# The last 96 rows of w_down move from ACT's queue at the start to Sync's queue behind load 17, in three loads on 16, 5 and 3 DMA engines

## The chip, the cores and the metric

The kernel runs on one core of a Trainium2 chip. The core has five engines with an instruction stream each: PE (matmuls; its weight loads are shown as PEld), DVE (vector work), ACT (scalar functions), POOL, and SP, here called Sync, which only issues transfers. Sixteen DMA engines move the data between memory (HBM) and the core's on-chip memory (SBUF). To keep the two kinds apart, the sixteen are always called DMA engines.

The metric is the device time of one execution in microseconds (us), the median over several runs.

## The reference

One decoding step for two rows of x (B = 2, D = 512). The rows are normalised (layernorm without weights), and three things are added: x itself, an attention over the last 2048 cached positions of 32 heads, and a gated linear block.

```python
x = A_x
xn = _layernorm(x, axis=-1)
# attention: q = xn @ wq per head; k, v = the last W = 2048 rows of the caches
scores = jnp.einsum("bhqd,bhkd->bhqk", q, k) * (Dh ** -0.5)
p = _softmax(scores, axis=-1)
o = jnp.einsum("bhqk,bhkd->bhqd", p, v)          # then @ wo
# linear block, F = 1376
h = (xn @ w_gate) * (xn @ w_up)
y = h @ w_down
return x + attention + y
```

All is float32. The caches alone are 2 x 32 x 2048 x 128 x 4 bytes for k and as much for v, 134 MB; with the weights the kernel reads 159 MB, and each byte is used once.

w_down has 1376 rows of 512 numbers (2 KB each). They are used in ten blocks of 128 rows and a rest of 96 rows. The change is about this rest, 196 608 bytes.

## The kernel before

**The stream.** The host lays caches and weights out as one long array, in the order in which the kernel wants them. The function `loads()` lists what is in each load: load 0 (constants and the first part of wq), load 1 (k of heads 0 to 2 and wq), load 2 (w_gate and w_up), loads 3 to 22 (three tiles of k or v each, 16 KB per partition, and up to three pieces of wq, wo or w_down), load 23 (v of head 30) and load 24 in five parts (v of head 31, pieces of wo, and w_down's blocks 1 to 9). A full load is 128 partitions of 13 824 numbers, 6912 KB. They go into three buffers `step0` to `step2` in turn; loads 0 and 23 go into `extra`.

**What sets the order.** A small recorder (`Program`) notes every operation with what it writes and reads; `emit` then writes each engine's instructions in the order in which the code named them, and adds the semaphore waits. There is no scheduler. Every operation is therefore recorded at one line, L198 of the profile (L197 for separate waits), and tiles, not lines, tell the operations apart.

All loads are issued on Sync, in the order of `queue`. `issue(n)` issues everything in the queue up to load n; a load waits on Sync until its buffer's last readers are done. Each DMA engine works off its own shares of the queued loads in order. Each load has a semaphore of its own.

**The steps.** For each head k is multiplied by q on DVE (`step<-step,q`, 4.4 us) and summed on DVE (`s<-step`, 4.4 us); for each group of four heads `weights` forms the softmax's weights (`mt`, `both`, `tr`, `nm`, `p`), and PE multiplies v with them (`o_ps<-step,p`). When a group is done, ACT copies its sums (`o_sb`), PE gathers them (`gu<-cst,o_sb`), DVE scales them (`oT`), and PE multiplies them with wo into `acc`. The loop `for n in range(3, 21)` does this load by load. `turn` (in step 3) puts the linear block's h into `hT`, 128 values to a column; PE multiplies its columns with the blocks of w_down, some in the loop and most at the very end, while load 24's parts land.

**The rest of w_down.** It has a buffer of its own, `wr`, 96 partitions of 512 numbers. It is loaded from a separate array, `wd_rest`, by ACT, right after Sync's first four loads have been recorded; behind it ACT issues the load of `xr`, the two rows of x as they are (2 partitions of 512). The product of `wr` with the last 96 values of h (`acc<-wr,hT`) is in `turn`.

Of the kernel before, what the change touches and what calls it, by code (L numbers as in the profile page):

```python
# [10 lines left out]
P = 128  # L11
B, D, H, DH, SK, F = 2, 512, 32, 128, 8192, 1376
# [7 lines left out]
NFC = F // P  # L20
FR = F - NFC * P
# [9 lines left out]
BUFS = 3  # L31
WIDTH = 13824
WIDTH_X = 4096


def loads():
# [199 lines left out]
def build(nc, stream, x_nat, wd_rest, out):  # L236
    pr = Program(nc)
    pe, dve, act, pool = pr.pe, pr.dve, pr.act, pr.pool

    buf = [pr.sb(f"step{i}", [P, WIDTH]) for i in range(BUFS)]  # L240
    buf_x = pr.sb("extra", [P, WIDTH_X])
    xr = pr.sb("xr", [P, D])
    wr = pr.sb("wr", [FR, D])
# [20 lines left out]
    hT = pr.sb("hT", [P, 4, NFB, B])  # L264
# [10 lines left out]
    got, used, queue, pos = {}, {}, [], 0  # L275
    for n, t, fields in loads():
        tile = buf_x if t == "x" else buf[t]
        c0 = used.get(n, 0)
        for kind, i, w in fields:
            c = used.get(n, 0)  # L280
            got[kind, i] = tile[:, c : c + w]
            used[n] = c + w
        c1 = used[n]
        assert c1 <= tile.shape[1], (n, c1)
        src = stream[pos : pos + P * (c1 - c0)].rearrange("(p i) -> p i", p=P)
        pos += P * (c1 - c0)
        queue.append((n, tile[:, c0:c1], src))

    def issue(upto):
        while queue and queue[0][0] <= upto:  # L290
            _, dst, src = queue.pop(0)
            pr.load("SP", dst, src)

    issue(3)
    pr.load("ACT", wr, wd_rest)
    dve.memset(mean_w, 1.0 / D)
    dve.memset(eps_t, EPS)
    dve.memset(ones, 1.0)
# [55 lines left out]
    def products(h):  # L354
        g, hh = divmod(h, HG)
        kt, qb = keys(h), q_ps[g % 2][:, hh * DH : (hh + 1) * DH]
        dve.tensor_tensor(kt, kt, qb.unsqueeze(1).to_broadcast([P, J, DH]), op=ALU.mult)

    def sums(h):
        g, hh = divmod(h, HG)  # L360
        dve.tensor_reduce(s_t[g % 2][:, hh, :], keys(h), axis=AX.X, op=ALU.add)
# [29 lines left out]
    def denominators(g):  # L391
        dve.tensor_reduce(
            rs, own(p_all[:, g % 2, 0, 0, 0:4], (HG, B, JG, 4)), axis=AX.XY, op=ALU.add
        )

    def reciprocals(g):
        dve.reciprocal(rec[g % 2], tot)

    def weigh(h, bank=None, first=None, last=None):
        g, hh = divmod(h, HG)  # L400
        bank = g % 2 if bank is None else bank
        first = hh == 0 if first is None else first
        last = hh == HG - 1 if last is None else last
        v = got["v", h]
        for i in range(JG):
            j = 32 * (i % 4)
            pe.matmul(
                o_ps[bank][j : j + M, :], p_all[:, g % 2, hh, i, :],
                v[:, i * FB : (i + 1) * FB],
                start=(first and i < 4), stop=(last and i >= JG - 4),  # L410
            )

    def fold(g):
        act.copy(o_sb[g % 2], o_ps[g % 2])

    def gather(g, lo=0, hi=N):
        for r in range(4):
            pe.matmul(
                pk_ps[:, lo:hi], o_sb[g % 2][:, r * DH : (r + 1) * DH], pick[:, r, lo:hi],
                start=(r == 0), stop=(r == 3),  # L420
            )

    def scaled(g, lo=0, hi=N):
        dve.tensor_tensor(
            oT[g % 2][:, lo:hi], pk_ps[:, lo:hi], rec[g % 2][:, lo:hi], op=ALU.mult
        )
# [5 lines left out]
    def add_rows(lhsT, rhs, j, last=False):  # L432
        pe.matmul(
            acc[32 * j : 32 * j + B, :], lhsT, rhs, start=(n_acc[j] == 0), stop=last
        )
        n_acc[j] += 1
# [33 lines left out]
    def turn():  # L470
        dve.tensor_copy(
            hT.rearrange("p i n b -> p (i n b)"), hT_ps[:, 0 : 4 * B * NFB]
        )
        add_rows(hT[:FR, NFC % 4, NFC // 4, :], wr, 0)

    def down(c, add, *args, **kw):
        add(hT[:, c % 4, c // 4, :], got["wd", c], *args, **kw)

    def wo(h, add, *args, **kw):
        g, hh = divmod(h, HG)  # L480
        add(oT[g % 2][:, B * hh : B * hh + B], got["wo", h], *args, **kw)
# [16 lines left out]
    def has(n, kind):  # L498
        return [i for k, i, _ in plan.get(n, []) if k == kind]
# [19 lines left out]
    def projections(done):  # L519
        while open_q and (open_q[0][1][0] - 2) * HG + HG - 1 <= done:  # L520
            project(*open_q.pop(0)[1])

    for n in range(3, 21):
        ks, vs = has(n, "k"), has(n, "v")
        for h in late_wo:
            wo(h, add_rows, h % HG)
        late_wo = []
        full = None
        for h in vs:
            if n > 3:  # L530
                weigh(h)
            if h % HG == HG - 1:
                full = h // HG
                fold(full)
        open_q += [(n, i) for i in has(n, "wq")]
        projections(ks[0] - 1)
        for c in has(n, "wd"):
            down(c, add_rows, 1)
        if full is not None:
            gather(full)  # L540
        for x, h in enumerate(ks):
            products(h)
            if open_g is not None:
                denominators(open_g)
                open_g = None
            if n == 3 and x == 0:
                turn()
            projections(h)
            sums(h)
            if n == 20 and x == 1:  # L550
                weigh(25)
                weigh(26)
            if h % HG == HG - 1:
                weights(h // HG)
                open_g = h // HG
                if open_g:
                    reciprocals(open_g - 1)
            if x == 0 and full is not None:
                scaled(full)
                for i in range(full * HG, full * HG + HG):  # L560
                    if i in has(n, "wo") or i in has(n - 1, "wo"):
                        wo(i, add_rows, i % HG)
                    else:
                        late_wo.append(i)
        if n == 3:
            weigh(vs[0])
        if n < 20:
            issue(min([n] + [m - 1 for m, _ in open_q]) + 3 + (n == 19))

    g = NG - 1  # L570
    a, b, c, d = GROUPS[g]
# [31 lines left out]
def laid_out(x):  # L603

    import numpy as np

    a = x["A_x"].reshape(B, D)
    xs = np.zeros((P, CX), a.dtype)
    xs[:, : B * NC] = a.reshape(B, P, NC).transpose(1, 0, 2).reshape(P, B * NC)
    o = B * NC  # L610
    for r in range(4):
        for n in range(N):
            xs[4 * n + r :: 32, o + r * N + n] = 1.0
    o += 4 * N
    for n in range(HG):
        for q in range(4):
            xs[32 * q + n, o + 4 * n + q] = 1.0
    o += 4 * HG
    for n in range(NFB):
        for b in range(B):  # L620
            xs[32 * n + b, o + n * B + b] = 1.0
    o += 2 * NFB
    for j in range(4):
        for b in range(B):
            xs[32 * j + b, o + b] = 1.0
    xs[:, o + 2 :] = a[:, 0]
    cache = {
        kind: x[name][:, :, SK - W :, :].reshape(B, H, HB, J * DH).transpose(1, 0, 2, 3)
        for kind, name in (("k", "A_k_cache"), ("v", "A_v_cache"))
    }  # L630
    wq = x["A_wq"].reshape(P, NC, H * DH)
    wo = x["A_wo"].reshape(H, P, D)
    gu = {
        kind: x[name].reshape(P, NC * F)
        for kind, name in (("wg", "B_w_gate"), ("wu", "B_w_up"))
    }
    wd = x["B_w_down"]

    def field(kind, i):
        if kind == "c":  # L640
            return xs
        if kind in ("k", "v"):
            return cache[kind][i].reshape(P, CK)
        if kind == "wq":
            g, c = i
            return wq[:, c, g * HG * DH : (g + 1) * HG * DH]
        if kind == "wo":
            return wo[i]
        if kind == "wd":
            return wd[i * P : (i + 1) * P]  # L650
        return gu[kind]

    parts = [
        np.concatenate([field(kind, i) for kind, i, _ in fields], axis=1).ravel()
        for _, _, fields in loads()
    ]
    return {"stream": np.concatenate(parts), "x": a, "wd_rest": wd[NFC * P :]}


_INS = ["A_x", "A_k_cache", "A_v_cache", "A_wq", "A_wo", "B_w_gate", "B_w_up", "B_w_down"]  # L660
# [24 lines left out]
```

## Time and profile before

| | |
|---|---|
| median of 3 runs | 377.47 us (377.38 to 377.53) |
| the profiled execution | 377.64 us |
| its span, first to last instruction | 376.3 us |
| moved by DMA in the span | 159.66 MB, mean 424 GB/s |
| busy: PE, DVE, ACT, POOL | 189.3, 302.8, 14.5, 2.6 us |
| load of `wr`: size, issue to landing | 192 KB, 5.5 us |
| a full load: issue to landing (median of 17) | 31.2 us |

The profile is that of one execution. Its 0 is the first instruction's start. In the timeline a row has start, duration, engine, line, operation, written tile, read tiles, shape, count, and in brackets the engine's idle time ahead of it with what ended it; `SPq` and `ACTq` are the queues' issuing instructions. In the chain of waits a row has start, duration and what the end of the kernel was waiting for in that time. The DMA view of a window counts the packets that start in it, by size and by queue; a queue's row has packets, MB and the time that its packets took as a share of 16 DMA engines over the window. A DMA engine that has finished its share of a load writes 4 bytes, and these count as packets too.

### The profile page before, as it was taken

What the parts mean: (1) busy time and instruction counts of PE and PEld (TensorE: products, weight loads), DVE (VectorE), ACT (ScalarE), POOL (GpSimd) and SP (SyncE); (2) the same over time, 40 slices, a digit from 0 to 9 for tenths busy, and PEclk for the clock granted to TensorE, in tenths of its full rate; (3) what the DMA queues carried; (4) which work ended last, traced back from release to release, by engine and by line L of the source; (5) the groups of instructions that cost most, each with busy time, mean ns of one, the idle gap of its engine ahead of it and who ended that gap; (6) DMA issues with size and microseconds to landing.
All of it is one profiled execution on the core that took longest, in us unless ns stands there. A gap on an engine that the chain in (4) does not pass through costs nothing.

```text
span 376.3 us, 1954 instructions
## 1 busy us (share of the span) xinstructions
PE 189.3 (50%) x844; PEld 56.8 (15%) x844; DVE 302.8 (80%) x165; ACT 14.5 (4%) x28; POOL 2.6 (1%) x9
## 2 busy tenths in 40 slices
PE   0651747703762355617446383462657335243976
PEld 0210122100220011102121020110111012000312
DVE  3059979999999988899599499969969997999401
ACT  1000100000000000000000000000000001000100
POOL 2000000000000000000000000000000000000000
PEclk9956966876665658768555856858566685565999
DMA  8999899998999989999999999999999999999995
GB/s 324 470 394 488 376 470 411 431 470 377 464 435 417 464 382 460 453 400 464 394 448 453 406 458 400 447 454 406 453 420 419 445 447 434 441 402 411 432 416 235
DMA packets 4443, 159.66 MB, mean 424 GB/s; under 512 B 498, under 2 KB 626, under 8 KB 980
## 3 DMA queue, kind: packets, MB, share of 16 engines
q1 hardware_dynamic: 4320, 159.35, 98.5%
q10 hardware_dynamic: 116, 0.20, 0.1%
q8 instruction: 6, 0.10, 0.1%
q14 instruction: 1, 0.01, 0.0%
HBM read 159.49 MB, written 0.07 MB: 424 GB/s over the span
## 4 chain that ended last, share of the span: by engine, by line
DMA 49%; DVE 42%; PE 6%; issue 2%; another core or an unknown queue 1%; SPq 0%; DVEq 0%
DMA step<-in_stream_dram 49%; DVE step L198 22%; DVE s L198 19%; PE q L198 3%; PE o_ps L198 2%; PE acc L198 2%; PE tr L198 0%; DVE both L198 0%; DVE nm L198 0%; DVE h_sb L198 0%; DVE rec L198 0%; SPq L198 0%; DVE mt L198 0%; DVE o_out L198 0%
## 5 line engine op out<-in xcount | busy, mean ns | idle before, releaser
L198 DVE TENSOR_TENSOR step<-step,q 128x4096 f32<-128x4096 f32 x32 | 141.1, 4408 | 37.3 <-DMA step<-in_stream_dram 37.3
L198 DVE TENSOR_REDUCE s<-step 128x32 f32<-128x4096 f32 x32 | 141.4, 4418 | 0.8
L198 PE MATMUL o_ps<-step,p 128*32 128x512 f32 x496 | 94.8, 869 | 69.8 <-DMA step<-in_stream_dram 68.2
L198 PE MATMUL q<-step,xnb 128*128 128x512 f32 x56 | 41.4, 877 | 26.9 <-DVE step L198 19.7
L198 PE MATMUL acc<-step,oT 128*2 128x512 f32 x64 | 23.6, 926 | 42.2 <-DVE oT L198 28.5
L198 PEld LDWEIGHTS o_ps<-step,p 128*32 128x32 f32 x496 | 20.4, 147 | 126.8 <-DMA step<-in_stream_dram 74.9
L198 PEld LDWEIGHTS q<-step,xnb 128*128 128x128 f32 x56 | 13.4, 267 | 54.5 <-DVE step L198 24.9
L198 ACT ACTIVATE p<-s,zero 64x128 f32<-64x128 f32 x16 | 6.4, 399 | 268.1 <-DVE s L198 268.0
L198 DVE TENSOR_TENSOR oT<-gu,rec 128x8 f32<-128x8 f32 x8 | 1.3, 158 | 14.8 <-PE gu L198 14.8
L198 PE MATMUL tr<-both,ones 128*128 128x24 f32 (+1 forms) x18 | 4.8, 348 | 15.7 <-DVE both L198 15.7
L198 PE MATMUL gu<-step,xn 128*2 128x512 f32 (+1 forms) x48 | 8.5, 647 | 7.5 <-DMA step<-in_stream_dram 7.5
L198 PE MATMUL gu<-cst,o_sb 128*128 128x8 f32 x64 | 10.1, 285 | 3.1 <-ACT o_sb L198 3.1
L198 PEld LDWEIGHTS gu<-cst,o_sb 128*128 128x128 f32 x64 | 9.4, 225 | 10.6 <-ACT o_sb L198 8.9
L198 PEld LDWEIGHTS acc<-step,oT 128*2 128x2 f32 x64 | 1.5, 82 | 53.0 <-DVE oT L198 29.1
L198 PEld LDWEIGHTS tr<-both,ones 128*128 128x128 f32 x18 | 3.8, 262 | 26.6 <-DVE both L198 26.6
L198 PE MATMUL q<-extra,xnb 128*128 128x512 f32 x8 | 6.2, 947 | 1.9 <-DVE xnb L198 1.9
L198 DVE TENSOR_REDUCE nm<-tr 64x4 f32<-64x8 f32 x16 | 2.6, 163 | 5.4 <-PE tr L198 5.3
L198 ACT COPY o_sb<-o_ps 128x512 f32<-128x512 f32 x8 | 4.7, 585 | 46.0 <-PE o_ps L198 46.0
L198 PE MATMUL gu<-cst,h_sb 128*128 128x6 f32 x8 | 1.9, 362 | 5.6 <-DVE h_sb L198 5.6
L198 PE MATMUL tr<-st,mean_w 128*128 128x4 f32 x2 | 0.6, 365 | 7.5 <-DVE st L198 7.5
L198 PEld LDWEIGHTS gu<-step,xn 128*2 128x2 f32 x48 | 2.0, 93 | 14.7 <-DMA step<-in_stream_dram 9.1
L198 DVE TENSOR_REDUCE both<-p 128x8 f32<-128x256 f32 x8 | 3.3, 413 | 0.6 <-ACT p L198 0.6
(52 smaller groups left out, 39.8 us busy)
## 6 DMA issues: line engine op xcount, KB each, us to landing
step<-in_stream_dram SPq DMA_DIRECT2D x17, 6912.0 KB, 31.2
step<-in_stream_dram SPq DMA_DIRECT2D x2, 6400.0 KB, 29.5
step<-in_stream_dram SPq DMA_DIRECT2D x1, 6656.0 KB, 35.9
step<-in_stream_dram SPq DMA_DIRECT2D x1, 5504.0 KB, 34.4
step<-in_stream_dram SPq DMA_DIRECT2D x1, 4608.0 KB, 23.8
extra<-in_stream_dram SPq DMA_DIRECT2D x1, 2048.0 KB, 28.3
step<-in_stream_dram SPq DMA_DIRECT2D x1, 2048.0 KB, 24.8
step<-in_stream_dram SPq DMA_DIRECT2D x2, 1024.0 KB, 19.6
```

Of the source, the lines that this page charges most:

```text
L198: ins = getattr(e, method)(*args, **kw)
```

## The change

The load of `wr` is taken from ACT. Behind load 17 three loads are put into Sync's queue instead: rows 0 to 31, viewed in memory as 16 times 2 rows, rows 32 to 56 as 5 times 5, and rows 57 to 95 as 3 times 13. The first dimension sets over how many DMA engines a load is spread. The host lays the rows out so that each lands in its old place. The product with `wr` is taken from `turn` and comes at step 19 of the loop, behind the products with v and ahead of the gather.

```diff
+REST_AT = 17
+REST = ((16, 32), (5, 25), (3, 39))
...
         queue.append((n, tile[:, c0:c1], src))
+        if n == REST_AT:
+            lo = 0
+            for k, m in REST:
+                src = wd_rest[lo : lo + m, :].rearrange("(j i) d -> i j d", i=k)
+                queue.append((n, wr[lo : lo + m, :], src))
+                lo += m
...
     issue(3)
-    pr.load("ACT", wr, wd_rest)
     dve.memset(mean_w, 1.0 / D)
...
         dve.tensor_copy(
             hT.rearrange("p i n b -> p (i n b)"), hT_ps[:, 0 : 4 * B * NFB]
         )
-        add_rows(hT[:FR, NFC % 4, NFC // 4, :], wr, 0)
...
         for c in has(n, "wd"):
             down(c, add_rows, 1)
+        if n == REST_AT + 2:
+            add_rows(hT[:FR, NFC % 4, NFC // 4, :], wr, 0)
         if full is not None:
             gather(full)
...
-    return {"stream": np.concatenate(parts), "x": a, "wd_rest": wd[NFC * P :]}
+    rest, lo = [], NFC * P
+    for k, m in REST:
+        rest.append(wd[lo : lo + m].reshape(k, m // k, D).transpose(1, 0, 2).reshape(m, D))
+        lo += m
+    return {"stream": np.concatenate(parts), "x": a, "wd_rest": np.concatenate(rest)}
```

Sync's transfers around load 17, before. The row with x15 ends with load 17; the rows under it are loads 18 to 21.

```order
L198 DMA step<-in_stream_dram 128x13824 x15
L198 DMA step<-in_stream_dram 128x12800
L198 DMA step<-in_stream_dram 128x13824
L198 DMA step<-in_stream_dram 128x12800
L198 DMA step<-in_stream_dram 128x13312
```

The same place after the change.

```order
L200 DMA step<-in_stream_dram 128x13824 x15
L200 DMA wr<-in_wd_rest_dram 32x1x512
L200 DMA wr<-in_wd_rest_dram 25x1x512
L200 DMA wr<-in_wd_rest_dram 39x1x512
L200 DMA step<-in_stream_dram 128x12800
```

Three loads of `wr` stand between loads 17 and 18, and none on ACT.

PE at step 19, before: the softmax's sums of step 18 (`tr`), step 19's products with v (`o_ps`), the gather (`gu<-cst,o_sb`), the products with wo (`acc<-step,oT`), and step 20's first products.

```order
L198 MATMUL tr<-both,ones 128x24
L198 MATMUL o_ps<-step,p 32x512 x8
L198 MATMUL gu<-cst,o_sb 128x8 x4
L198 MATMUL acc<-step,oT 2x512 x4
L198 MATMUL o_ps<-step,p 32x512 x24
```

The same place after the change.

```order
L200 MATMUL tr<-both,ones 128x24
L200 MATMUL o_ps<-step,p 32x512 x8
L200 MATMUL acc<-wr,hT 2x512
L200 MATMUL gu<-cst,o_sb 128x8 x4
L200 MATMUL acc<-step,oT 2x512 x4
```

The product with `wr`, one matmul of the program that the profile shows as two, stands between the products with v and the gather; in step 3 it is gone.

## The prediction

> **What bounds the kernel now.** I read the DMA queues first, then the chain of waits from its end backwards, then the DMA in small windows.
>
> ```profile
> q1 hardware_dynamic: 4320, 159.35, 98.5%
> q10 hardware_dynamic: 116, 0.20, 0.1%
> q8 instruction: 6, 0.10, 0.1%
> q14 instruction: 1, 0.01, 0.0%
> ```
>
> q1 is Sync's queue (packets, MB, share of the time of 16 DMA engines in the span): the stream fills 98.5%. q10 is ACT's: the 96 rows that are moved and the two rows of x. q8 and q14 fetch instructions: seven packets.
>
> The chain of waits, its later part (start, duration, who):
>
> ```profile
> 248.34 34.23 DMA step<-in_stream_dram
> ...
> 309.05 35.85 DMA step<-in_stream_dram
> ...
> 350.90 22.78 DMA step<-in_stream_dram
> 373.68 0.04 issue
> 373.72 0.66 PE q L198 x16
> 374.38 0.02 issue
> 374.41 0.29 DVE o_out L198
> ```
>
> The last load (512 KB) is issued at 350.90 and lands at 373.68: it stood 20 us in the queue. What follows is 16 matmuls, a copy and the store. So the end is set by the bytes queued on the DMA engines, provided the queue is never empty. The closest it comes to that is load 4, from the timeline:
>
> ```profile
> 44.56 5.29 SPq L198 DMA_DIRECT2D step<-in_stream_dram  x2
> 52.34 4.42 DVE L198 TENSOR_TENSOR step<-step,q 128x4096 f32<-128x4096 f32 x1 [2.25 <-DMA step<-in_stream_dram]
> ```
>
> Load 4 is issued at 44.56, and load 3 ahead of it lands only at 52.3 (DVE's wait ends there): 7.8 us of cover, the smallest of all loads. Nothing that the compute engines do within a microsecond moves the end.
>
> But "the queue" is sixteen. A load is cut into sixteen equal shares, and each DMA engine works off its own shares in order. Each reports a share with a 4-byte write, which the DMA view counts under "under 512 B". Four windows: around load 4's landing (67.70 to 68.25), two around that of load 24's first part (363.20 to 363.75, 364.60 to 365.20), and the last reports of all (372.60 to 373.30; the wait for them ends 0.4 us later, at 373.68):
>
> ```profile
> DMA packets 32, 0.88 MB, mean 1609 GB/s; under 512 B 16, under 2 KB 16, under 8 KB 16
> DMA packets 29, 0.22 MB, mean 402 GB/s; under 512 B 9, under 2 KB 9, under 8 KB 9
> DMA packets 34, 0.22 MB, mean 369 GB/s; under 512 B 7, under 2 KB 7, under 8 KB 7
> DMA packets 21, 0.06 MB, mean 82 GB/s; under 512 B 7, under 2 KB 7, under 8 KB 21
> ```
>
> At load 4 all sixteen report within half a microsecond. Late in the run nine report, and seven more come over a microsecond later. Seven is also the number of instruction packets above. The DMA view from 68 to 72 us shows one of these:
>
> ```profile
> q8 instruction: 1, 0.02, 1.7%
> ```
>
> 1.7% of 16 engines in 4 us is 1.09 us of one engine. Such a fetch pushes back one DMA engine's share for good, and since no packet of the stream ever waits for work, it never catches up. At the end the others idle (stretch, its length, then each engine's busy time; the last two numbers are the DMA share and GB/s):
>
> ```profile
> 361.00:362.00 1.00, 1.00 (x12) 0.26 (x8) 0.00 (x0) 0.00 (x0) 0.00 (x0) 1.00 0.96 410
> 371.25:371.50 0.25, 0.25 (x4) 0.00 (x0) 0.00 (x0) 0.00 (x0) 0.00 (x0) 1.00 1.05 426
> 371.50:372.00 0.50, 0.16 (x4) 0.00 (x0) 0.27 (x1) 0.00 (x0) 0.00 (x0) 1.00 0.50 197
> 372.00:372.50 0.50, 0.02 (x4) 0.03 (x8) 0.42 (x1) 0.00 (x0) 0.00 (x0) 1.00 0.42 172
> 372.50:373.00 0.50, 0.50 (x20) 0.48 (x24) 0.00 (x0) 0.00 (x0) 0.00 (x0) 1.00 0.34 139
> ```
>
> From 371.5 on the share is 0.50, 0.42, 0.34: seven engines of sixteen (0.44) carry the last 1.5 us. The time of the kernel is that of the latest DMA engine, not of the mean.
>
> **The change part by part.** Before, the 96 rows of 2 KB go out from ACT at the start, six to each DMA engine, between the packets of load 0. The timeline's row, and the queues from 2 to 7 us:
>
> ```profile
> 0.73 0.41 ACTq L198 DMA_DIRECT2D wr<-in_wd_rest_dram  x1
> DMA packets 263, 2.06 MB, mean 412 GB/s; under 512 B 34, under 2 KB 34, under 8 KB 132
> q10 hardware_dynamic: 116, 0.20, 11.3%
> ```
>
> q10's 116 packets are 96 + 2 rows and 16 + 2 reports, so x's load of two rows ran on two DMA engines. *Price of a row:* 11.3% of 16 engines in 5 us is 9.04 us, over 98 rows 0.092 us, with the reports and a small overlap in it: the upper bound. The lower is the bytes alone: 410 to 426 GB/s over 16 engines, quoted above, is 26 GB/s each, 0.077 us for 2 KB. I take 0.080, near the lower end, since single packet records put the next packet that long after a row's start.
>
> *New shares.* 32 rows on 16 engines are 2 each; 25 on 5 are 5; 39 on 3 are 13. If the small loads use the same end of the row of engines (an assumption; the only load on few engines before is x's), three engines get 2 + 5 + 13 = 20 rows, two get 7, eleven get 2. Against 6 each: +14 rows (+1.12 us), +1 row (+0.08 us), -4 rows (-0.32 us). [...]
>
> *Who is late.* Followed from packet to packet (on one engine the next begins 3 or 4 ns before the one ahead ends), the records of the two engines that carry x's rows show no instruction fetch. They are among the nine: they make their last report at about 371.66 and 371.80, the latest engine at 373.24. With +1.12 the later of them ends at 372.92. The latest engine, if it is not favoured, ends at 373.24 - 0.32 = 372.92. Both put the end 0.32 earlier. With 0.092 a row the favoured engine ends at 373.09 and the gain is 0.15; with 0.077 it is 0.31. I take 0.31.
>
> *The start.* All engines begin the stream without six rows between load 0's packets: loads 0 to 17 land 0.48 us earlier, which pays nothing by itself, since the rows come back behind load 17. Sync's issues (shortest, median, longest, ns):
>
> ```profile
> L198 SPq DMA_DIRECT2D step<-in_stream_dram x27: 327/328/679, 1.2 to 350.9; - x27
> ```
>
> Three more of these are 1.0 to 2.0 us of Sync, right behind load 17's issue, without a wait and with the queue covered by at least 7.8 us: free, and without that cover 2 us late. ACT issues one less.
>
> *The product moves* from the turn of h in step 3 to step 19. There it must wait for all three loads, and the gather stands behind it on PE. Timeline, step 3 (three rows) and step 19 (four rows):
>
> ```profile
> 56.91 1.86 PE L198 MATMUL acc<-wr,hT 96*2 96x512 f32 x2 [2.47 <-DVE hT L198]
> 62.04 0.23 DVE L198 TENSOR_SCALAR both<-cst,mc 128x16 f32<-128x16 f32 x1
> 62.33 0.62 PE L198 MATMUL tr<-both,ones 128*128 128x24 f32 x2
> ...
> 314.08 3.64 PE L198 MATMUL o_ps<-step,p 128*32 128x512 f32 x16 [3.32 <-DMA step<-in_stream_dram]
> 317.79 0.58 ACT L198 COPY o_sb<-o_ps 128x512 f32<-128x512 f32 x1 [5.48 <-PE o_ps L198]
> 318.43 1.88 PE L198 MATMUL gu<-cst,o_sb 128*128 128x8 f32 x8 [0.70 <-ACT o_sb L198]
> 323.05 0.15 DVE L198 TENSOR_TENSOR oT<-gu,rec 128x8 f32<-128x8 f32 x1
> ```
>
> In step 3 PE is rid of 1.86 us ahead of a product that waits for DVE until 62.27 anyway: at most 0.1 us of DVE's time, and none at the end. In step 19 the rows have landed for some 30 us (load 17, ahead of them, lands at 282.6 by the chain). The product takes up to 1.86 us from 317.8; 0.70 of it is PE's idle time, so the gather ends 1.2 us later, near 321.5; DVE, busy until 323.05, is what the next step waits for. Free, with 1.5 us of cover; without it 1.2 us late on DVE, which has 7.8 us to the DMA.
>
> *Sum.* -0.31 for the shares, 0 for the start, the issues and the product. The profiled execution took 377.64 (span 376.3), 0.17 above the median; the same difference on the median of 377.47 gives 377.16, on the profiled execution 377.33.
>
> **A rule against the change.** The last parts of load 24 land back to back in PE's waits, and the store shows a lone small transfer:
>
> ```profile
> 360.76 1.92 PE L198 MATMUL o_ps<-extra,p 128*32 128x512 f32 x16 [1.27 <-DMA extra<-in_stream_dram]
> 365.65 1.93 PE L198 MATMUL o_ps<-step,p 128*32 128x512 f32 x16 [1.26 <-DMA step<-in_stream_dram]
> out_dram<-o_out SPq DMA_DIRECT2D x1, 64.0 KB, 1.6
> ```
>
> 2048 KB in 365.65 - 360.76 = 4.89 us is 429 GB/s: a load behind another pays no fixed time. If each small load did block its engines for the store's 1.6 us, the three engines that serve all three loads would end 4.8 - 0.48 = 4.3 us later and the kernel, less their 1.44 us of room, some 2.9 us: 380.4. [...] The row of 429 GB/s speaks against it for queued loads.
>
> **The rivals.**
> *The third favoured engine is a late one (slower).* x shows two of the three engines. The third is one of the other fourteen, seven of which are late. By their last reports (372.74 to 373.24) plus 1.12 the end would be 373.86 to 374.36: 0.62 to 1.12 later, 378.1 to 378.6, over the bound of change from about +0.75. It decides as soon as that engine has had a fetch. For it: by count alone 7 in 14. Against it: the seven fetches hit seven different engines, which chance would do in one of five cases, so they go round in an order; q8's six on neighbours that spare the first two engines have nine places to begin, one of which includes the third, and q14's one falls on it once in fourteen. I give it 0.15.
> *Little or nothing is gained.* One of the two engines with 7 rows is a late one: it ends at 372.82 to 373.32, and the kernel at 377.16 to 377.55. 0.08.
> *Each small load has a fixed price*, 380.4: 0.03.
> *More is gained.* The stream's opening (2.06 MB in 5 us) is held up by ACT's rows for more than their bytes, up to another half microsecond: 376.6. Against it: 412 GB/s there is what the stream does later. 0.05.
>
> **How the numbers follow.** Forecast 377.16 with 0.69; its own range, by the price of a row and the spread of the times shown (377.38 to 377.53), is 377.0 to 377.4. The range for 8 in 10 reaches to the lower part of the first rival: 376.9 to 378.1. A measurement of this kernel can tell about 0.2% (0.75 us) from no change, so the forecast counts as no change. Faster: the last rival, and a little more for its mechanism beside the forecast's, 0.07. Slower: three quarters of the first rival (five of the seven late engines are late enough) and the fixed price, 0.15. Within: 0.78.
>
> **What would show it.** After the change, load 0's wait on DVE ends about 0.4 us earlier; q10 has 4 packets instead of 116; behind load 17 Sync issues three loads of wr; from 371.5 on the DMA share stays near 1 for longer and falls within some 0.2 us, with the last report near 372.9. If the third engine is late, one engine alone reports a microsecond behind the others and the share ends in a tail of 0.06. If the rows cost more, three engines are last. The forecast is wrong if an instruction fetch lands on a favoured engine, or if a load on three engines does not use x's two.

## The result: 0.56 us slower, small but clear of the noise, and the profile after

| | before | after |
|---|---|---|
| median of 21 runs | 377.47 us (377.32 to 377.72) | 378.03 us (377.74 to 378.32) |
| the profiled execution | 377.64 us | 377.83 us |

The ratio is 1.0014, with a 95% interval from 1.0008 to 1.0020. The interval lies above 1, so the kernel is slower, by about 0.15%. The profiled execution of after is one of its shorter ones, 0.20 below its median, and that of before 0.17 above its own, so the two traces differ by 0.19 us where the medians differ by 0.56. What is read below are parts of the traces that differ by a microsecond.

The queues of the changed kernel (packets, MB, share):

```profile
q1 hardware_dynamic: 4440, 159.55, 98.7%
q8 instruction: 6, 0.10, 0.1%
q14 instruction: 1, 0.01, 0.0%
q10 hardware_dynamic: 4, 0.00, 0.0%
```

The rows have left ACT's queue, which has x's four packets. Sync's has 120 more, 96 rows and 24 reports, and 24 is 16 + 5 + 3: the loads ran on as many DMA engines as their first dimensions have. The fetches are still seven. The end of the chain of waits, after:

```profile
351.04 22.81 DMA step<-in_stream_dram
373.85 0.04 issue
373.89 0.66 PE q L200 x16
374.55 0.02 issue
374.58 0.29 DVE o_out L200
```

The end has the same form as before and the last load lands at 373.85 instead of 373.68. The timeline's waits for loads 0, 15, 17 and 18, before:

```profile
6.64 0.20 DVE L198 COPY cst<-extra 128x66 f32<-128x66 f32 x1 [3.83 <-DMA extra<-in_stream_dram]
...
249.90 4.42 DVE L198 TENSOR_TENSOR step<-step,q 128x4096 f32<-128x4096 f32 x1 [3.55 <-DMA step<-in_stream_dram]
...
282.59 4.42 DVE L198 TENSOR_TENSOR step<-step,q 128x4096 f32<-128x4096 f32 x1 [3.34 <-DMA step<-in_stream_dram]
...
297.73 1.94 PE L198 MATMUL o_ps<-step,p 128*32 128x512 f32 x8 [7.79 <-DMA step<-in_stream_dram]
```

And the same four, after:

```profile
5.75 0.20 DVE L200 COPY cst<-extra 128x66 f32<-128x66 f32 x1 [2.94 <-DMA extra<-in_stream_dram]
...
248.91 4.42 DVE L200 TENSOR_TENSOR step<-step,q 128x4096 f32<-128x4096 f32 x1 [3.55 <-DMA step<-in_stream_dram]
...
282.55 4.42 DVE L200 TENSOR_TENSOR step<-step,q 128x4096 f32<-128x4096 f32 x1 [4.29 <-DMA step<-in_stream_dram]
...
297.87 1.94 PE L200 MATMUL o_ps<-step,p 128*32 128x512 f32 x8 [9.07 <-DMA step<-in_stream_dram]
```

A row's start is the landing of the load it waited for. Without the rows the start is 0.89 us earlier (6.64 to 5.75), and load 15 still 0.99 us. At load 17 the lead has shrunk to 0.04, and at load 18 after is 0.14 behind. So all that the start gave, and a little more, is lost around the rows' new place. The 8 us around it, before and then after (length, busy time of PE, PEld, DVE, ACT, POOL, then PE's clock, DMA share, GB/s):

```profile
276.00:284.00 8.00, 4.33 (x22) 1.51 (x26) 4.66 (x3) 0.11 (x1) 0.00 (x0) 0.62 1.00 432
```

```profile
276.00:284.00 8.00, 2.74 (x14) 0.54 (x18) 3.71 (x3) 0.00 (x0) 0.00 (x0) 0.68 0.93 343
```

The DMA engines are busy in both (1.00 and 0.93), but they move 343 GB/s instead of 432. A packet counts with all its bytes where it starts, so such a window is rough: begun a microsecond later it gives 392 against 420. The landings above say more exactly what is lost. The DMA engines have work nearly throughout (1.03 from 277 to 287 us); their packets take longer.

The tail of after, and the last reports of all (the DMA view from 373.05 to 373.50):

```profile
371.50:372.00 0.50, 0.32 (x4) 0.00 (x0) 0.12 (x1) 0.00 (x0) 0.00 (x0) 1.00 0.83 336
372.00:372.50 0.50, 0.00 (x0) 0.00 (x0) 0.50 (x1) 0.00 (x0) 0.00 (x0) 1.00 0.69 279
372.50:373.00 0.50, 0.37 (x16) 0.36 (x20) 0.08 (x1) 0.00 (x0) 0.00 (x0) 1.00 0.64 262
373.00:373.50 0.50, 0.50 (x28) 0.38 (x16) 0.00 (x0) 0.00 (x0) 0.00 (x0) 1.00 0.27 107
```

```profile
DMA packets 21, 0.05 MB, mean 100 GB/s; under 512 B 10, under 2 KB 10, under 8 KB 21
```

The share stays high for longer than the 0.50, 0.42, 0.34 of before, and ten DMA engines report last, within 0.45 us: the seven that had a fetch, and three with 20 rows each (from the packet records, followed one after another on each DMA engine). The balance is the computed one; it is reached later.

Single packet records show what slowed. Each group is of one size, so that a longer time is not more bytes (ns; from the records, which the views sum up):

```
                                   before       after         without rows anywhere (first experiment)
load 0's packets, 8456 B, median      370         320         320
a row's packet, 2048 B, median         84         127         -
load 18's first packet on each of
the 16 DMA engines, 51 200 B    1891-1898   2042-2885   1891-1898
```

Before, the rows begin at 2.7 us. Beyond each DMA engine's first packet, load 0's packets still take 320 ns for the first microsecond beside the rows, and some 320 to 400 ns from 3.75 us on. Without rows they stay at 320. After, every one of the sixteen DMA engines has a slow packet behind load 17, also the eleven that carry only two rows.

### The profile page after: what moved, and what is told of

Read it like the earlier page. It is cut to its first block, busy times and chain, and to the rows that moved or that the text cites. A ratio compares the mean times of both kernels' runs of the same rounds, so it can differ in the third digit from the quotient of the medians.

```text
span 376.5 us, 1956 instructions
## 1 busy us (share of the span) xinstructions
PE 187.2 (50%) x844; PEld 55.5 (15%) x844; DVE 302.8 (80%) x165; ACT 14.5 (4%) x28; POOL 2.6 (1%) x9
## 4 chain that ended last, share of the span: by engine, by line
DVE 49%; DMA 48%; PE 2%; SPq 1%; issue 0%
DMA step<-in_stream_dram 48%; DVE s L200 24%; DVE step L200 23%; PE acc L200 1%; DVE both L200 1%; PE tr L200 1%; SPq L200 1%; DVE mt L200 0%; DVE nm L200 0%; DVE mtt L200 0%; DVE mc L200 0%; PE q L200 0%; DVE rec L200 0%; DVE oT L200 0%; DVE o_out L200 0%
## 5 line engine op out<-in xcount | busy, mean ns | idle before, releaser
L200 PE MATMUL o_ps<-step,p 128*32 128x512 f32 x496 | 96.9, 888 | 70.2 <-DMA step<-in_stream_dram 68.6
L200 PE MATMUL q<-step,xnb 128*128 128x512 f32 x56 | 38.6, 823 | 31.5 <-DVE step L200 23.6
L200 PE MATMUL gu<-step,xn 128*2 128x512 f32 (+1 forms) x48 | 9.4, 712 | 8.1 <-DMA step<-in_stream_dram 8.1
L200 PE MATMUL gu<-cst,o_sb 128*128 128x8 f32 x64 | 9.3, 271 | 2.4 <-ACT o_sb L200 2.4
L200 PEld LDWEIGHTS gu<-cst,o_sb 128*128 128x128 f32 x64 | 8.6, 208 | 9.8 <-ACT o_sb L200 8.0
```

The lines of the kernel that those rows point to most:

```text
L200: ins = getattr(e, method)(*args, **kw)
```

## The experiments

Each run is set against the kernel before on the same chip, whose median was 377.50, 377.52 and 377.51 in the three groups. Two readings serve: the median, and, for rows that come behind load 17, the time from load 15's landing to load 18's, from waits like those above (before, with no rows there, 297.73 - 249.90 = 47.83; after 297.87 - 248.91 = 48.96). The table at the end of this section has both.

### What the rows cost at all

Without the three loads and the product.

```diff
-        if n == REST_AT:
+        if False:
...
-        if n == REST_AT + 2:
-            add_rows(hT[:FR, NFC % 4, NFC // 4, :], wr, 0)
```

> The changed kernel without the three loads of wr and without their product (the last 96 values of h are left out of the result). It gives the floor: what the 96 rows cost in either place. If rows cost only their own 0.08 us each (the prediction's price, 6 to a DMA engine), the time is 0.48 under the kernel before: 377.0. If they also hold up the stream beside them by what load 0 showed (its reports came 0.75 to 0.83 us earlier without them), it is 376.65 to 376.7.

Measured: 376.72 (376.66 to 377.00), ratio 0.9978 [0.9969, 0.9987].

```profile
5.74 0.20 DVE L200 COPY cst<-extra 128x66 f32<-128x66 f32 x1 [2.92 <-DMA extra<-in_stream_dram]
...
248.98 4.42 DVE L200 TENSOR_TENSOR step<-step,q 128x4096 f32<-128x4096 f32 x1 [3.33 <-DMA step<-in_stream_dram]
...
281.65 4.42 DVE L200 TENSOR_TENSOR step<-step,q 128x4096 f32<-128x4096 f32 x1 [3.33 <-DMA step<-in_stream_dram]
...
296.80 2.79 PE L200 MATMUL o_ps<-step,p 128*32 128x512 f32 x12 [7.58 <-DMA step<-in_stream_dram]
```

This is the floor. Up to load 15 it goes like after; load 17 lands 0.90 and load 18 1.07 us earlier. The rows' own bytes, 196 608 at the stream's 424 GB/s, are 0.46 us if all engines share them. They cost 377.50 - 376.72 = 0.78 at the start and 378.03 - 376.72 = 1.31 behind load 17. In both places they cost more than their bytes, and the records above show packets beside them that are slowed.

### Where the source lies in memory

The first idea for it: 96 neighbouring rows of 2 KB are one small region of memory, on which all engines read at once. Here the rows lie 55 296 B apart, in after and in before.

```diff
-                src = wd_rest[lo : lo + m, :].rearrange("(j i) d -> i j d", i=k)
+                src = wd_rest[lo : lo + m, 0:D].rearrange("(j i) d -> i j d", i=k)
...
+    rows = np.concatenate(rest)
+    apart = np.zeros((FR, WIDTH), rows.dtype)
+    apart[:, :D] = rows
```

> As the changed kernel, but in memory each row of wd_rest stands 55 296 bytes from the next instead of 2048. Theory A (rows close together in memory: DMA engines that read them at once are held up at one place, and the stream's reads with them): the rows go back to 84 ns each, the stream's packets beside them to 1.9 to 2.05 us, and the time falls by about 0.9 to 377.1. Theory B (the rows' destination: partitions that other DMA engines write) and theory C (any run of 2 KB packets slows the DMA engines): nothing changes, 378.0.

Measured: 378.04 (377.87 to 378.14), ratio 1.0013 [1.0004, 1.0021]; the rows' packets still take up to 167 ns.

```diff
-    pr.load("ACT", wr, wd_rest)
+    pr.load("ACT", wr, wd_rest[:, 0:D])
...
+    apart = np.zeros((FR, WIDTH), wd.dtype)
+    apart[:, :D] = wd[NFC * P :]
```

> The kernel before, but in memory each row of wd_rest stands 55 296 bytes from the next. Theory A: load 0's packets beside the rows stay at 320 ns instead of 380, load 0 lands 0.3 us earlier, and the time is 377.1 to 377.2. Theories B and C: 377.47.

Measured: 377.53 (377.42 to 378.13), ratio 1.0003 [0.9994, 1.0012]. Both stay where they were: how close the rows lie in memory is not it.

### One load on sixteen engines

Perhaps the loads on few DMA engines did it. The same 96 rows, behind load 17, as one load of six rows to each engine:

```diff
-REST = ((16, 32), (5, 25), (3, 39))
+REST = ((16, 96),)
```

> As the changed kernel, but the 96 rows behind load 17 are one load on 16 DMA engines, six rows each. Theory A: the rows are still close together, but three DMA engines no longer read neighbouring rows in step: it is held up as at the start of the kernel before, 377.4 to 377.6. Theory C: 96 small packets as before, 377.5. If it is the few DMA engines with many rows each that do the harm: only 6 x 0.08 = 0.48 over the floor, 377.1 to 377.2.

Measured: 378.22 (377.89 to 378.47), ratio 1.0018 [1.0009, 1.0027]. None of the expectations was near it. It is no better than the three loads, so spreading over few engines is not what costs. One transfer is not cheaper than three, as a fixed price for each load would make it; that it is 0.19 dearer is not clear of the noise, since the two intervals overlap.

### Who writes which partitions

Left were the destination and small packets as such. A load of the stream always has 128 partitions; this one has 96. With 128 rows, 32 of them zero, the load has the stream's 128 partitions. That each DMA engine then writes the partitions that it writes in the stream is the author's assumption, and no trace shows it.

```diff
-    wr = pr.sb("wr", [FR, D])
+    wr = pr.sb("wr", [P, D])
...
-            lo = 0
-            for k, m in REST:
-                src = wd_rest[lo : lo + m, :].rearrange("(j i) d -> i j d", i=k)
-                queue.append((n, wr[lo : lo + m, :], src))
-                lo += m
+            queue.append((n, wr, wd_rest))
```

> The rest of w_down behind load 17 as one load of 128 rows of 2 KB (the 96, and 32 rows of zeros, 64 KB more) to all 128 partitions, in the natural order, so that it has the stream's own shape. Theory A is out, since rows apart in memory cost as much. Theory B (rows that a DMA engine writes to other partitions than those it writes in the stream hold up all): each DMA engine now writes the partitions that it writes in the stream, so nothing is held up; 8 rows of 0.08 us over the floor of 376.72 is 377.36. Theory C (2 KB packets as such slow the DMA engines): 128 of them do at least what 96 did, 378.0 to 378.4.

Measured: 377.39 (377.14 to 377.45), ratio 0.9996 [0.9987, 1.0005].

```profile
248.79 4.42 DVE L200 TENSOR_TENSOR step<-step,q 128x4096 f32<-128x4096 f32 x1 [3.56 <-DMA step<-in_stream_dram]
...
281.48 4.42 DVE L200 TENSOR_TENSOR step<-step,q 128x4096 f32<-128x4096 f32 x1 [3.34 <-DMA step<-in_stream_dram]
...
297.31 1.93 PE L200 MATMUL o_ps<-step,p 128*32 128x512 f32 x8 [9.05 <-DMA step<-in_stream_dram]
```

```profile
276.00:284.00 8.00, 3.68 (x18) 0.79 (x22) 4.66 (x3) 0.00 (x0) 0.00 (x0) 0.68 1.02 434
```

A third more rows, and 0.64 us less than after. Load 17 isn't held up (281.48 - 248.79 = 32.69, as in before, against 33.64 in after), the 8 us keep 434 GB/s, and all 128 row packets take 84 to 88 ns. So packets of 2 KB as such are not slow. The cost, 377.39 - 376.72 = 0.67, is about what 262 144 B take at 424 GB/s, 0.62.

The same 128 rows as 512 more columns of load 18, so that there is no extra load:

```diff
-        18: wq(7, 3),
+        18: wq(7, 3) + units("wd", 10),
```

> The same 128 rows (32 of zeros), but as 512 more columns of load 18, so that they are part of its packets of 51 200 bytes, which become 53 248: no packet of 2 KB and no load of its own. Theories B and C alike: 8 x 2 KB at the stream's rate, 0.60 to 0.64 over the floor, 377.3 to 377.4. If more, it is neither the rows' destination nor their size but the bytes at this place.

Measured: 377.32 (377.22 to 377.39), ratio 0.9995 [0.9986, 1.0003], a cost of 0.60: the extra load itself costs next to nothing.

And the 128 rows in the kernel before, at the start on ACT:

```diff
-    wr = pr.sb("wr", [FR, D])
+    wr = pr.sb("wr", [P, D])
...
+    rest = np.zeros((P, D), wd.dtype)
+    rest[:FR] = wd[NFC * P :]
```

> The kernel before, with the load of wr on ACT at the start as 128 rows (32 of zeros) to 128 partitions. Theory B: no packet of load 0 is held up (320 ns all through), 8 x 0.08 over the floor: 377.36, under the kernel before although it moves 64 KB more. Theory C: 0.78 x 128 / 96 = 1.04 over the floor, 377.76.

Measured: 377.31 (377.16 to 377.65), ratio 0.9996 [0.9987, 1.0005], a cost of 0.59 where the 96 rows cost 0.78. The interval holds 1, so the times alone don't tell the two apart; the trace does.

```profile
6.34 0.20 DVE L198 COPY cst<-extra 128x66 f32<-128x66 f32 x1 [3.53 <-DMA extra<-in_stream_dram]
```

With a third more bytes the first wait ends 0.30 us earlier than before's 6.64, and nearly all of load 0's packets stay at 320 ns.

128 rows differ from 96 in the number of rows too. This run keeps the 128 rows, their packets and their place behind load 17, and changes the view by which they are dealt out: 16 times 8, by which each DMA engine should be given eight neighbouring partitions. The host stores the rows in another order to match, so that each lands in its old place.

```diff
-            queue.append((n, wr, wd_rest))
+            src = wd_rest.rearrange("(j i) d -> i j d", i=16)
+            queue.append((n, wr, src))
```

> As the kernel with one load of 128 rows behind load 17 (377.39), with one difference: its source is viewed as 16 times 8 rows, as the change views its first load, so that each DMA engine should take 8 partitions in a row instead of those that it writes in the stream. Same bytes, same packets, same partitions in all. Theory B (a DMA engine that writes other partitions than in the stream holds up all): rows take up to 180 ns, the packets beside them lose about 1 us, as with 96 rows in one load (1.5 over the floor of 376.72), 378.2 to 378.6. If the shape of the load is not what matters: 377.39.

Measured: 378.43 (378.12 to 378.72; 8 runs), ratio 1.0026 [1.0016, 1.0037].

```profile
248.94 4.42 DVE L200 TENSOR_TENSOR step<-step,q 128x4096 f32<-128x4096 f32 x1 [3.56 <-DMA step<-in_stream_dram]
...
282.43 4.42 DVE L200 TENSOR_TENSOR step<-step,q 128x4096 f32<-128x4096 f32 x1 [4.14 <-DMA step<-in_stream_dram]
...
298.49 1.08 PE L200 MATMUL o_ps<-step,p 128*32 128x512 f32 x4 [9.24 <-DMA step<-in_stream_dram]
```

```profile
276.00:284.00 8.00, 3.51 (x15) 0.54 (x18) 3.86 (x3) 0.00 (x0) 0.00 (x0) 0.54 0.96 351
```

This is the clean pair: 1.04 us lie between two kernels that move the same bytes in the same packets. Load 17 is held up again (33.49), the rate is 351 GB/s, the row packets have a median of 124 ns and reach 185, and load 18's first packets take 2066 to 2824 ns. What should differ by the two views is which DMA engine gets which rows: the partitions that it writes, and the places in memory that it reads. The runs with rows apart in memory speak against the second (378.04 against 378.03 of after, 377.53 against 377.50 of before). The two ran on different chips, on which the kernel before had medians of 377.52 and 377.51.

So the partitions that a DMA engine writes are the likely reason: in the natural order nothing is held up, in blocks of eight the rows and the stream's packets are (377.39 against 378.43). But a packet's record doesn't name its partitions, neither in these loads nor in the stream, so this is the author's reading and not a shown one.

### Unequal shares, to partitions 4 apart

If that is right, the arithmetic of shares should hold once the rows go to partitions that their engine writes anyway. Here the shares are still unequal, with 84 of the 96 rows: 32 rows as 128 pieces of 512 B on all sixteen DMA engines, 4 KB for each, then 25 rows on five, and 21 and 6 on three, so that three DMA engines get the bytes of 16 rows if the loads on few take the same ones, as in after. (The DMA view from 279 to 283 us has 43 reports: 16 of load 17, and 16 + 5 + 3 + 3.) All go to another buffer, and the product is left out. The loads on few DMA engines go to partitions 4 apart, one for each of them. The author took these for partitions which the DMA engine writes in the stream too; that is an assumption, and no trace shows it.

```diff
+            queue.append((n, buf_x[:, 7 * D : 7 * D + P], wd_rest[:32].rearrange("r (a d) -> (r a) d", a=4)))
+            for k, m, p0, c in ((5, 25, 32, 0), (3, 21, 0, 0), (3, 6, 32, 5 * D)):
+                src = wd_rest[32 : 32 + m, :].rearrange("(j i) d -> i j d", i=k)
+                dst = buf_x[p0 : p0 + 4 * k : 4, c : c + m // k * D]
+                queue.append((n, dst.rearrange("i (j d) -> i j d", d=D), src))
```

> [...] Theory B: nothing is held up, the late DMA engines get 4 KB each (0.16 over the floor of 376.72), and the three favoured ones, with 16 rows or 1.28 us, stay ahead of the late ones: 376.9. So the prediction's arithmetic of shares would hold once the destination is right. If unequal shares hold up the stream by themselves: 377.8 to 378.0, as in the changed kernel.

Measured: 376.92 (376.88 to 377.02), ratio 0.9986 [0.9977, 0.9995].

```profile
248.93 4.42 DVE L200 TENSOR_TENSOR step<-step,q 128x4096 f32<-128x4096 f32 x1 [3.55 <-DMA step<-in_stream_dram]
...
281.66 4.42 DVE L200 TENSOR_TENSOR step<-step,q 128x4096 f32<-128x4096 f32 x1 [3.38 <-DMA step<-in_stream_dram]
...
297.00 2.79 PE L200 MATMUL o_ps<-step,p 128*32 128x512 f32 x12 [8.93 <-DMA step<-in_stream_dram]
```

Load 17 isn't held up (32.73), and the whole costs 0.20 over the floor, where two rows on a late engine are 2 x 0.080 = 0.16. So loads on five and three engines, and views of three dimensions, did no harm here. The run has fewer rows and another buffer than after, so it is not a pair that differs in one thing.

### Does the place matter

The one load of 96 rows, behind load 4 instead of 17:

```diff
-REST_AT = 17
-REST = ((16, 32), (5, 25), (3, 39))
+REST_AT = 4
+REST = ((16, 96),)
```

> One load of the 96 rows on 16 DMA engines behind load 4 instead of load 17, when all DMA engines are in step (no instruction fetch yet); its product is taken in step 6. If the harm behind load 17 comes from DMA engines that are out of step (late ones still in load 17 while others are at the rows), it is less here: as at the start of the kernel before, 377.4 to 377.6. Theories B and C, which know nothing of the place: 378.2, as behind load 17.

Measured: 377.74 (377.33 to 377.94), ratio 1.0006 [0.9997, 1.0014]. The cost is 1.02, between the 0.78 of the start and the 1.50 behind load 17. The stream's packets beside the rows take 2200 to 2585 ns instead of 2041 to 2044. Neither expectation was met, and the premise of one did not hold: the first instruction fetch starts at 67.09 us, beside the rows (66.78 to 69.01). The load costs more behind load 17 than behind load 4 (the runs' ranges, from 377.89 and up to 377.94, barely touch); that it costs more behind load 4 than at the start is not clear of the noise, since the interval holds 1. The fetches put the DMA engines more and more out of step (in the trace of before sixteen report within half a microsecond at load 4, and at the first part of load 24 seven come over a microsecond after nine), and rows of one that meet the stream of another for longer would do this; that is argued, and no run separates it from what else differs between the places (at the start it is ACT's queue, too).

### The 96 rows packed into a load of the stream

If rows in the stream's own shape cost only their bytes, the cheapest whole form is 96 rows packed into 128 partitions: 384 columns more in load 18, rows 0 to 95 with their first 384 numbers, and the remaining 128 numbers of each in partitions 96 to 127. The product becomes one matmul of 96 partitions and three of 32.

```diff
+CW, CL = FR * D // P, D - FR * D // P
...
-        18: wq(7, 3),
+        18: wq(7, 3) + units("wr", 0),
...
+    def rest():
+        w, n = got["wr", 0], NFC // 4
+        pe.matmul(acc[0:B, 0:CW], hT[:FR, NFC % 4, n, :], w[:FR, :], start=False, stop=False)
+        for g in range(3):
+            pe.matmul(
+                acc[0:B, CW:D], hT[FR:, 4 + g, n, :], w[FR:, g * CL : g * CL + CL],
+                start=False, stop=False,
+            )
```

> The 96 rows without zeros in load 18: 384 more columns of all 128 partitions (rows' columns 0 to 383 on partitions 0 to 95, the last 128 columns of all rows on partitions 96 to 127), four smaller products instead of one, and three more small products ahead of turn. Theory B: 192 KB at the stream's rate, 12 288 bytes to each DMA engine, 0.46 over the floor of 376.72: 377.18, 0.14 under the kernel with 32 rows of zeros in load 18 (377.32). If the small products of turn or of step 18 come onto the path: over 377.4.

Measured: 377.15 (377.04 to 377.33), ratio 0.9991 [0.9982, 1.0000]. It is 0.88 faster than after and 0.36 faster than before, and costs 0.43, about the 0.46 us of its bytes. Against before that is at the edge of what can be told apart.

### All of them

Cost is the median less 376.72 (the median of before moved by 0.05 between the groups, and 377.50 is that of the first). The last column is the landing of load 18 less that of load 15, and in brackets what that is over the 47.82 of the kernel without rows.

| rows | median, us | cost, us | load 15 to load 18, us |
|---|---|---|---|
| none | 376.72 | 0 | 47.82 (0) |
| unequal shares, partitions 4 apart (84 rows) | 376.92 | 0.20 | 48.07 (0.25) |
| 96 packed in load 18 | 377.15 | 0.43 | 48.28 (0.46) |
| 128 at the start | 377.31 | 0.59 | |
| 128 in load 18 | 377.32 | 0.60 | 48.61 (0.79) |
| 128 behind load 17 | 377.39 | 0.67 | 48.52 (0.70) |
| before: 96 at the start | 377.50 | 0.78 | 47.83 (0.01) |
| 96 in one load behind load 4 | 377.74 | 1.02 | |
| after: 96 in three loads behind load 17 | 378.03 | 1.31 | 48.96 (1.14) |
| the same, source rows apart | 378.04 | 1.32 | 48.98 (1.16) |
| 96 in one load behind load 17 | 378.22 | 1.50 | 49.39 (1.57) |
| 128 in blocks of eight behind load 17 | 378.43 | 1.71 | 49.55 (1.73) |

Where the rows come behind load 17 or in load 18, the median over runs and the one stretch of one trace agree within 0.2 us. So what is lost is lost at that place and stays lost to the end.

The packet records say what the loss is made of. Near the rows, add up how much longer the rows and the stream's packets take than such packets do where nothing holds them up (84 ns for a row, 320, 1894 and 2044 ns for the stream's 8456, 51 200 and 55 296 B), and divide by 16: this is the *stretch*, a mean for each DMA engine. To it comes what the rows of a late engine take by themselves, at 0.084 us each (us; one trace each, cost from the medians):

```
rows                              own time      stretch   sum    cost
before: 96 at the start           6 rows 0.50    0.28     0.78   0.78
96 in one load behind load 4      6 rows 0.50    0.42     0.92   1.02
96 in one load behind load 17     6 rows 0.50    1.10     1.60   1.50
after: three loads                2 rows 0.17    1.02     1.19   1.31
128 behind load 17                8 rows 0.67    0.03     0.70   0.67
128 in blocks of eight            8 rows 0.67    1.13     1.80   1.71
```

The sums come within 0.12 us of the costs. In after the stretch is 16.3 us of DMA engine time, of which the rows' own packets have 3.3; the rest is the stream's.

## Why the prediction was wrong, step by step

*What bounds the kernel* held. The end is still the last report of the latest DMA engine, seven of them late by their fetches (of after's seven, six take 1.02 to 1.07 us and one 0.33); the time lost around load 17 goes through to the end undiminished.

*New shares* and *Who is late* held: three engines with 20 rows, among them both that carry x's rows, and none of the three with a fetch, so the third-engine rival did not come. One of the two engines with 7 rows did have a fetch, as the rival *Little or nothing is gained* had it, but no single engine sets the end: ten report within 0.45 us. The recorded sign that three engines alone would be last if rows cost more did not come either, since every engine was held up.

*Price of a row* is the step that failed. It bounded a row by its own packet, 0.077 to 0.092 us, and charged it to the engine that carries it. What it left out, without a reason, is what the rows do to the stream's packets on all sixteen engines: the stretch, 1.02 us for each engine in after against 0.28 in before. In the trace of before some of this was to be seen: load 0's packets took 320 ns at first and up to 400 later beside the rows. The lower and the upper bound both left that out, since both were taken from the rows. By the price taken, two rows on a late engine are 0.16 over a kernel without rows; after has 1.31. In the run with unequal shares and partitions 4 apart it is 0.20, so the arithmetic of shares held there, where load 17 was not held up.

*The start* was mis-sized by the same step: 0.48 was forecast, and in the two traces the loads land 0.89 (load 0) to 0.99 us (load 15) earlier; over the runs, the rows at the start cost 0.78. The rival *More is gained* had this mechanism, that ACT's rows hold the opening up for more than their bytes, and counted it as a gain alone. It did not ask whether the rows would do the same at the place to which they go, and there they do more: 1.31 against 0.78.

*Sum*: -0.31 was forecast, +0.56 measured. The forecast's loss, 0.16 over the floor against 0.48 before, becomes 1.31 against 0.78.

*Sync's issues* held: they are free.

```profile
247.34 0.33 SPq L200 DMA_DIRECT2D step<-in_stream_dram  x1
247.71 2.43 SPq L200 DMA_DIRECT2D wr<-in_wd_rest_dram  x3
```

Three issues take 2.43 us, more than the 2.0 of the estimate's upper end, some 30 us ahead of what they fetch.

*The product* held. Step 19, after:

```profile
317.63 1.91 PE L200 MATMUL acc<-wr,hT 96*2 96x512 f32 x2
...
319.47 1.88 PE L200 MATMUL gu<-cst,o_sb 128*128 128x8 f32 x8
323.19 0.16 DVE L200 TENSOR_TENSOR oT<-gu,rec 128x8 f32<-128x8 f32 x1
```

The gather starts 1.04 us later than before (318.43) and ends at 321.35, near the 321.5 of the forecast; DVE comes to `oT` at 323.19 as it would have anyway.

*The rule against the change*, a fixed price for each small load, did not show: one load of 128 rows costs about its bytes (0.67 against 0.62), and three loads were not dearer than one (378.03 against 378.22).

*How the numbers follow* took 0.2% (0.75 us) for what a measurement can tell from no change. The 21 runs tell 0.06%, and they show a slowdown where a gain of 0.31 was forecast. The measured 378.03 lies inside the range given by luck: its upper part was made for a late third engine, and what came is a mechanism that none of its cases held at the rows' new place.

## What to carry to other kernels

Price a transfer beside a full stream by what the stream's packets do next to it, not by its own packets: compare packets of one size with and without it beside them. Give such a transfer the stream's own shape, all 128 partitions in their natural order, even if a quarter of it is zeros, or pack it into one of the stream's loads; here it then cost about its bytes (0.67, 0.60 and 0.43 us, against 0.62, 0.62 and 0.46). Unequal shares did no harm in the one run whose loads on few DMA engines went to partitions 4 apart (0.20 us); no run shows a whole kernel that gains by them.

## What was not expected of the hardware

A few rows of 2 KB can hold up all sixteen DMA engines: in after, with 96 of them in three loads, packets of 51 200 B rise from 1891 to as much as 2885 ns, and 0.20 MB take as long as 0.56 MB would (1.31 us at 424 GB/s). The same 128 rows cost 0.67 us in the natural order and 1.71 in blocks of eight. How far apart the rows lie in memory makes no difference (378.03 and 378.04). That it is the partitions written is the likely reading, and no trace names them. How a few rows slow every engine stays open, and so does why the same 96 rows, six to an engine, cost 0.78 at the start, 1.02 behind load 4 and 1.50 behind load 17.
